# Where layer 1's second half loads its two wide tiles of x: in its tenth and thirteenth gate and up pass

## The chip, the cores and the metric

The kernel runs on one core of a Trainium2 chip. The metric is the device time of one execution in microseconds (us), of which several runs are made; their median counts. The engines are TensorE (PE), VectorE (DVE), ScalarE (ACT), GpSimd (POOL) and SyncE (SP); transfers go over 16 DMA engines, issued here mostly by SyncE ("SPq" in the profile is its queue) and by GpSimd.

## The reference

Four layers act on x, 2048 x 512 in float32, each with a norm of the rows in front and the old x added behind. Layers 0 and 2 mix by Fourier matrices, layers 1 and 3 are a gated feed-forward block with a hidden width of 1792:

```python
def _A_ref(x, dft_seq_re, dft_seq_im, dft_hid_re, dft_hid_im):
    a = jnp.einsum("bsd,ed->bse", x, dft_hid_re)
    b = jnp.einsum("bsd,ed->bse", x, dft_hid_im)
    return jnp.einsum("ts,bse->bte", dft_seq_re, a) - jnp.einsum("ts,bse->bte", dft_seq_im, b)

def _B_ref(x, w_gate, w_up, w_down):
    return (_gelu(x @ w_gate) * (x @ w_up)) @ w_down

x = x + _A_ref(_layernorm(x), ...)
x = x + _B_ref(_layernorm(x), w_gate, w_up, w_down)
x = x + _A_ref(_layernorm(x), ...)
x = x + _B_ref(_layernorm(x), w_gate, w_up, w_down)
```

## The kernel before

Every product is made of three matmuls of 128x128 by 128x512 (mm3, L213 to L215): an operand is split into a high part, which ScalarE rounds (L156), and a low part, which VectorE gets by subtraction (L158). Blocks of two by two are multiplied by Strassen's scheme (Winograd's form) with seven products instead of eight, so VectorE also adds and subtracts blocks (L189 in `minus`, L193 and L196 in `plus`), ScalarE copies finished banks of PSUM (L200 in `copied`) and writes a block into a bank as the start of a sum (L207 in `seed`). There are eight banks, p0 to p7, and 98 slots of SBUF, s0 to s97, each 128x512; both are handed out and given back as the program is written.

**Rows and layers.** x is kept in DRAM after each layer in four quarters of 512 rows: x1_2 is what layer 0 left (it is layer 1's input) of quarter 2, x2_0 what layer 1 left of quarter 0. A feed-forward layer runs in two halves (w = 0 and 1) of two quarters each. A half has 14 gate and up passes (n = 0 to 13, the function `up`), about 10 us each, in which the products of the down matrix are begun beside them (`beside`), and then the remaining down products (`down_product`, the loop over `late`). Layer 1's second half starts near 608 us, its passes end near 748, and layer 2 begins near 780. While its passes run, the norms of layer 2's rows are made ahead (`terms_ahead`): a row of x2_0 or x2_1 is loaded (L241, queue of SyncE), ScalarE sums it and its squares (L614 to L616), GpSimd takes the power (L617, L618) and ScalarE the shift (L619); later the row is loaded again and normed (L640).

**The wide tiles.** The down products come out transposed. Their result is added to x in a tile that holds a quarter of x in blocks of 32x32, turned: `xwide` for the half's first quarter (part 0, from the pool `upool`, one buffer) and `wide` for its second (part 1, from `tpool`, one buffer). `load_turned(part)` takes the tile and fills it by four loads of 256 KB on SyncE (L1508), each of 32 partitions by 16 by 128 floats, in runs of 512 bytes. `turned_into` (L801) adds a product into it on VectorE (L196), first into `xwide`, and `rows_done` writes the tile to the next layer's x.

In the program's text `load_turned(0)` is called by `beside(13)` in the last pass (k is the last pair there), and, where all seven pairs use Strassen's scheme for the down product, once more after the passes. So layer 1's halves and the first half of layer 3 load `xwide` twice with the same data: the second load waits only for the first one to land. `load_turned(1)` is called a third of the way through `late`.

**What sets the order.** The text is not the order of issue. A scheduler walks the program with its own model of time and puts an instruction on its engine's queue as soon as what it needs and the room it writes are free by that model, unless it is held by `tc.issue_after(i)`, which puts it behind the instruction i. A load needs only room, so the loads of the wide tiles go as soon as their single buffers are free, long before the place in the text. The weights are a stream of items with a look-ahead: `AHEAD` of 7 items are split ahead of use, and four more raw ones are loaded (`load_next`, L327 to L335, which notes its newest load as `stream["last"]`). On each engine, SyncE's queue among them, the instructions then run strictly in the scheduler's order. The loads of SyncE take eight completion semaphores in turn, so one is issued when the eighth before it has landed.

Of the kernel before, what the change touches and what calls it, by code (L numbers as in the profile page):

```python
# [29 lines left out]
LAG = 6  # L30
NEAR = 3, 2, 6
EARLY = 2
EARLY_FROM, EARLY_EACH = 8,2
PACE = 9
SKEW = 2, 1
# [17 lines left out]
def fnet_geglu(ctx: ExitStack, tc: tile.TileContext, x_in, ws, wh, wgu, wdn, wdc, whc, out):  # L53
# [32 lines left out]
    nc = tc.nc  # L86
# [111 lines left out]
    def copied(src):  # L198
        v = sb.get()
        bank_read["ACT"] = nc.scalar.activation(v, src, AF.Copy)  # L200
        return v
# [121 lines left out]
    stream = {"loaded": 0, "split": 0, "used": 0, "more": 0}  # L323
# [24 lines left out]
    def take():  # L348
        n = stream["used"]
        while stream["split"] < len(items):  # L350
            at = stream["split"]
            _, _, make, need = items[at]
            if too_far(at) or make is not whole and at > n + AHEAD + stream["more"]:
                break
            if make is not whole and need and need not in cs and at > n:
                break
            split_next()
        stream["used"] += 1
        return parts.pop(n)
# [126 lines left out]
    NP = NF // 2  # L486
# [308 lines left out]
    def moved(wide, outside, run):  # L795
        view = outside.rearrange("(j t) (p e) -> p t j e", t=32, e=P)
        for p in range(NT):
            v = wide[p * 32:(p + 1) * 32]
            run(v.rearrange("t (j e) -> t j e", e=P), view[p])
# [458 lines left out]
    def geglu(w, layer):  # L1258
# [12 lines left out]
        def ready(f, part):  # L1271

            t = h.get((f, part))
            if t is not None and not isinstance(t, tuple):
                h[f, part] = split_slot(t)
                sb.put(t)

        def down_steps(f, part):
# [3 lines left out]
            v = take()  # L1282
            for k in range(EARLY + 1):
                ready(f + k, part)
# [17 lines left out]
        def product(n, ps, an, bn, start, stop):  # L1302
            step()
            hi, lo = wparts[n][an]
            for c in range(2):
                cut = slice(c * P, (c + 1) * P)
                mm3(ps, (hi[:, cut], lo[:, cut]), blocks[bn, c], start and c == 0, stop and c == 1)
            if n == NF - 1:
                for c in range(2):
                    sb.put(*blocks.pop((bn, c)))  # L1310
            if an in ends:
                i = ends[an]
                sb.put(*wparts[n][i])
                if not making and n + 2 < NF:
                    piece_load(n + 2, i)
# [15 lines left out]
        def beside_mix(n):  # L1331
            run = spare.pop(0) if spare and (layer > 1 or n >= 1) else None
            if run:
                run()

        def beside_next(n, down):
            beside_mix(n)
            next(down, None)

        def up(n):  # L1340
            if n + 3 in making:
                making[n + 3][0]()
            if n + 2 in making:
                queue.extend(making[n + 2][1])
            if n > 2 or w:
                for _ in range(DOWN_RUNS[3]):
                    run = down_making.pop(0) if down_making else None
                    if run:
                        run()
            product(n, chain[n], "S2", "T2", False, True)  # L1350
            u[n] = copied(chain[n])
            down = beside(n)
            beside_next(n, down)
            side[n] = ps8.get()
            product(n, side[n], "S1", "T1", True, True)
            w4[n] = copied(side[n])
            beside_next(n, down)
            first(n + 1)
            beside_mix(n)
            product(n, chain[n], "S3", "T3", False, True)  # L1360
            v = w4.pop(n)
            plus(v, v, chain[n])
            finished(n, 1, 1, v)
            sb.put(v)
            beside_next(n, down)
            product(n, side[n], "S4", "B22", False, True)
            v = u.pop(n)
            plus(v, v, side[n])
            ps8.put(side.pop(n))
            finished(n, 0, 1, v)  # L1370
            sb.put(v)
            beside_next(n, down)
            second(n + 1)
            if pairs == NP:
                for name, k in down_order(layer, w)[1][:max(0, n - EARLY_FROM) * EARLY_EACH]:
                    if k in h4:
                        prepared(name, k)
            product(n, chain[n], "A22", "T4", False, True)
            ps = chain.pop(n)
            if n % 2 == 0:  # L1380
                v = copied(ps)
                finished(n, 1, 0, v)
                sb.put(v)
            else:
                finished(n, 1, 0, ps)
            ps8.put(ps)
            beside_next(n, down)
            for _ in down:
                pass
# [15 lines left out]
        pairs = SEVEN.get((layer, w), 0)  # L1405
# [73 lines left out]
        def beside(n):  # L1479

            if plain_down:
                return down_steps(n - LAG, 0) if n >= LAG else iter(())
            k = (n - 1) // 2
            if k >= pairs:
                return iter(())
            if n % 2:
                if k == pairs - 1:
                    load_turned(0)
                bs["A11", k] = split_slot(h[2 * k, 0])
                return down_product("A11", k)  # L1490
            if n:
                pair_combined(k)
                return down_product("A12", k)
            return iter(())

        xturned, begun = {}, {}
# [4 lines left out]
        def outside(at, part):  # L1501
            return begun[part] if at == layer + 1 and pairs < NP else xs[at, w * 2 + part]

        def load_turned(part):
            assert part or not sb.out("x")
            pool = tpool if part else upool
            xturned[part] = pool.tile([P, NT * D], F32, name="wide" if part else "xwide")
            moved(xturned[part], outside(layer, part), lambda v, rows: nc.sync.dma_start(v, rows))  # L1508

        def turned_rows(part, c, src):  # L1510
            turned_into(xturned[part], c, src)
# [15 lines left out]
        def load_rows(part):  # L1527
            xrows.extend(x_load(layer, (w * 2 + part) * NT + i) for i in range(NT))
# [72 lines left out]
                slow.pop(0)()  # L1601
        if plain_down:
            load_rows(0)
        elif pairs == NP:
            load_turned(0)
        if w == 0:
            queue.extend([None] * 9 + others[len(ahead_of_all):ND] + ([] if ahead_of_all else [None] * 4) + others[ND:])
# [3 lines left out]
        if plain_down:  # L1611
            for f in range(NF - LAG, NF):
                down(f, 0)
            add_rows(0)
            if before_mix:
                for k in range(NT):
                    queue.extend([lambda k=k: second_rows(layer + 1, k), lambda k=k: combine(k)])
                queue.extend([lambda k=k: combine_late(k) for k in range(NT)])
            else:
                queue.extend(ahead)  # L1620
            for f in range(NF):
                if f == NF - 2:
                    load_rows(1)
                down(f, 1)
                while len(queue) > 2 * (NF - 1 - f):
                    step()
            add_rows(1, before_mix)
        else:
            if pairs == NP:
                pair_combined(NP - 1)  # L1630
            late = down_order(layer, w)[1]
            for i, (name, k) in enumerate(late):
                if name == "S4" and pairs < NP:
                    break
                if pairs < NP and name == "S1" and k > 1:
                    prepared("S4", k - 2)
                for more in late[i:i + EARLY + 1]:
                    prepared(*more)
                for _ in down_product(name, k):
                    pass  # L1640
                if i == len(late) - HOLD:
                    late_end.append(newest["PE"])
                if not before_mix or i % 3 == 0:
                    step()
                if before_mix and i == len(late) // 2:
                    stream["more"] = MORE
                if i == len(late) // 3:
                    load_turned(1)
                    if w == 0:
                        queue[:2 * len(ahead)] = [run for pair in zip(ahead, queue) for run in pair] + queue[len(ahead):2 * len(ahead)]  # L1650
                while w == 0 and len(queue) > 2 * (len(late) - 1 - i):
                    step()
            if pairs < NP:
                fourth_products()
                plain_rows()
# [120 lines left out]
```

## Time and profile before

| what | us |
|---|---|
| median of three runs | 1599.49 |
| the runs | 1596.91, 1599.49, 1601.11 |
| the profiled execution's own time | 1599.44 |
| its span in the profile | 1597.5 |
| VectorE busy, share of the span | 1176.7, 74% |
| ScalarE busy, share of the span | 890.4, 56% |

One execution was recorded. A row of a timeline is one instruction, or several alike in a row: when it starts, how long it takes, its line and what it does, and in brackets how long its engine had stood idle before it and what ended that. In a group, the same figures are summed over a line. A matmul is shown as 0.39 long but the next begins 0.23 after it, since they overlap. The chain of waits goes back from the last instruction of a stretch to what released each one. The mean rate of the DMA engines over the span is 270 GB/s, and the granted clock of TensorE is at its full value throughout (all slices of the page show 9 tenths or more).

### The profile page before, as it was taken

What the parts mean: (1) busy time and instruction counts of PE and PEld (TensorE: products, weight loads), DVE (VectorE), ACT (ScalarE), POOL (GpSimd) and SP (SyncE); (2) the same over time, 40 slices, a digit from 0 to 9 for tenths busy, and PEclk for the clock granted to TensorE, in tenths of its full rate; (3) what the DMA queues carried; (4) which work ended last, traced back from release to release, by engine and by line L of the source; (5) the groups of instructions that cost most, each with busy time, mean ns of one, the idle gap of its engine ahead of it and who ended that gap; (6) DMA issues with size and microseconds to landing.
All of it is one profiled execution on the core that took longest, in us unless ns stands there. A gap on an engine that the chain in (4) does not pass through costs nothing.

```text
span 1597.5 us, 22834 instructions
## 1 busy us (share of the span) xinstructions
PE 1589.7 (100%) x6984; PEld 1310.1 (82%) x6984; DVE 1176.7 (74%) x2042; ACT 890.4 (56%) x1731; POOL 293.6 (18%) x493
## 2 busy tenths in 40 slices
PE   9999999999999999999999999999999999999999
PEld 6888888888888888788888888888888888888887
DVE  8997878888689794665879867777895557844573
ACT  8955465754767653566648545556553565333460
POOL 4112121351457101330031000001301000000000
PEclk9999999999999999999999999999999999999999
DMA  9878888996998999997895876878978968895445
GB/s 363 290 264 295 305 307 280 356 309 202 316 363 315 278 323 294 350 361 238 290 299 187 272 242 213 271 247 249 257 257 277 273 213 256 296 295 173 132 145 158
DMA packets 249433, 431.74 MB, mean 270 GB/s; under 512 B 29344, under 2 KB 74656, under 8 KB 248288
## 3 DMA queue, kind: packets, MB, share of 16 engines
q1 hardware_dynamic: 220464, 340.36, 67.3%
q0 software_dynamic: 26160, 87.84, 15.3%
q10 hardware_dynamic: 2688, 2.10, 0.5%
q8 instruction: 55, 0.90, 0.2%
q14 instruction: 66, 0.54, 0.1%
HBM read 344.46 MB, written 85.72 MB: 269 GB/s over the span
## 4 chain that ended last, share of the span: by engine, by line
PE 90%; DMA 3%; issue 3%; ACT 2%; DVE 1%; POOL 1%; SPq 0%; POOLq 0%; ACTq 0%; DVEq 0%
PE p L214 30%; PE p L213 30%; PE p L215 30%; DMA s<-t 1%; ACT s L156 1%; DVE s L158 1%; PE p L999 1%; DMA xwide<-x 1%; DMA s<-x 1%; DMA s<-ws 0%; POOL rstd L617 0%; PE p L1682 0%; ACT s L200 0%; ACT p L207 0%; DVE s L189 0%
## 5 line engine op out<-in xcount | busy, mean ns | idle before, releaser
L214 PE MATMUL p<-s,s 128*128 128x512 f32 x2312 | 897.7, 389 | 0.8 <-DVE s L158 0.8
L215 PE MATMUL p<-s,s 128*128 128x512 f32 x2312 | 892.3, 389 | 0.0
L213 PE MATMUL p<-s,s 128*128 128x512 f32 x2312 | 858.2, 389 | 1.6 <-ACT p L207 1.5
L156 ACT ACTIVATE s<-s 128x512 fp32r<-128x512 f32 (+1 forms) x859 | 483.1, 608 | 266.1 <-DVE s L189 66.9
L158 DVE TENSOR_TENSOR s<-s,s 128x512 fp32r<-128x512 f32 (+1 forms) x859 | 540.1, 663 | 111.9 <-ACT s L156 94.8
L213 PEld LDWEIGHTS p<-s,s 128*128 128x128 f32 x2312 | 433.8, 188 | 93.6 <-ACT p L207 2.6
L214 PEld LDWEIGHTS p<-s,s 128*128 128x128 f32 x2312 | 433.9, 188 | 92.1 <-DVE s L158 2.3
L215 PEld LDWEIGHTS p<-s,s 128*128 128x128 f32 x2312 | 433.9, 188 | 90.4
L193 DVE TENSOR_TENSOR s<-s,p 128x512 f32<-128x512 f32 x199 | 134.7, 683 | 163.2 <-PE p L215 136.6
L189 DVE TENSOR_TENSOR s<-s,s 128x512 f32<-128x512 f32 (+1 forms) x415 | 245.1, 612 | 4.7 <-DMA s<-ws 2.2
L200 ACT ACTIVATE s<-p 128x512 f32<-128x512 f32 x232 | 134.4, 593 | 112.6 <-PE p L215 108.5
L1253 ACT ACTIVATE s<-s 128x512 f32<-128x512 f32 x84 | 52.8, 628 | 46.4 <-DVE s L193 46.1
L617 POOL TENSOR_SCALAR rstd<-rstd 128x1 f32<-128x1 f32 x40 | 23.2, 580 | 239.3 <-ACT s L616 231.5
L1253 ACT ACTIVATE s<-p 128x512 f32<-128x512 f32 x28 | 16.7, 596 | 83.2 <-PE p L215 83.2
L319 POOL DMA_DIRECT2D wb<-s x84 | 46.2, 552 | 91.2 <-ACT s L156 68.9
L640 ACT ACTIVATE s<-s,shift,rstd 128x512 f32<-128x512 f32 x59 | 47.6, 812 | 16.9 <-DVE shift L607 9.7
L1269 DVE TENSOR_TENSOR s<-s,p 128x512 f32<-128x512 f32 x56 | 38.3, 684 | 24.7 <-PE p L215 24.7
L158 DVE TENSOR_TENSOR s<-xwide,s 128x512 fp32r<-128x512 f32 (+1 forms) x49 | 32.8, 679 | 25.2 <-ACT s L156 25.2
L196 DVE TENSOR_TENSOR s<-s,s 128x512 f32<-128x512 f32 (+1 forms) x73 | 44.2, 613 | 6.8 <-DMA s<-ws 3.8
L207 ACT ACTIVATE p<-p 128x512 f32<-128x512 f32 x56 | 32.6, 584 | 24.2 <-PE p L215 23.9
L729 DVE STREAM_TRANSPOSE wide<-s 128x512 f32<-128x512 f32 x31 | 21.9, 708 | 25.8 <-ACT s L640 21.8
L1190 POOL DMA_DIRECT2D wc<-s x42 | 30.6, 730 | 54.0 <-ACT s L156 36.3
(104 smaller groups left out, 621.8 us busy)
## 6 DMA issues: line engine op xcount, KB each, us to landing
s<-ws SPq DMA_DIRECT2D x406, 256.0 KB, 5.0
s<-wb SPq DMA_DIRECT2D x294, 256.0 KB, 5.2
s<-wc SPq DMA_DIRECT2D x182, 256.0 KB, 4.6
wb<-s POOLq DMA_DIRECT2D x98, 256.0 KB, 5.2
s<-wh SPq DMA_DIRECT2D x84, 256.0 KB, 5.3
s<-x SPq DMA_DIRECT2D x53, 256.0 KB, 5.3
wc<-s POOLq DMA_DIRECT2D x49, 256.0 KB, 5.3
xwide<-ws SPq DMA_DIRECT2D x36, 256.0 KB, 4.9
```

The source lines that it names most:

```text
L156: newest["ACT"] = nc.scalar.activation(hi, src, AF.Copy)
L158: newest["DVE"] = nc.vector.tensor_tensor(lo, src, f32(hi), op=ALU.subtract)
L189: nc.vector.tensor_tensor(out, a, b, op=ALU.subtract)
L193: bank_read["DVE"] = nc.vector.tensor_tensor(out, a, b, op=ALU.add)
L196: nc.vector.tensor_tensor(out, a, b, op=ALU.add)
L200: bank_read["ACT"] = nc.scalar.activation(v, src, AF.Copy)
L213: nc.tensor.matmul(ps, ah, bh, start=start, stop=False, skip_group_check=True)
L214: nc.tensor.matmul(ps, ah, bl, start=False, stop=False, skip_group_check=True)
L215: newest["PE"] = nc.tensor.matmul(ps, al, bh, start=False, stop=stop, skip_group_check=True)
L319: nc.gpsimd.dma_start(a, f32(t))
L640: nc.scalar.activation(z, x, AF.Identity, bias=shift, scale=rstd)
L1253: nc.scalar.activation(t, g, AF.Gelu_apprx_tanh)
```

## The change

In the second half of layer 1, `load_turned(0)` is called in the tenth pass (n = 9) and `load_turned(1)` in the thirteenth (n = 12), by a new constant `TURNED`; there the loads are held behind the stream's newest weight load by `issue_after`. `beside(13)` still loads part 0 once more. After the passes, a part that has its tile is not loaded again: that takes four loads away in the first half of layer 1 and four in that of layer 3.

```diff
+TURNED = 9, 12
@@ up(n)
             beside_next(n, down)
+            if (layer, w) == (1, 1) and n in TURNED:
+                load_turned(TURNED.index(n))
             side[n] = ps8.get()
@@ load_turned(part)
             xturned[part] = pool.tile([P, NT * D], F32, name="wide" if part else "xwide")
-            moved(xturned[part], outside(layer, part), lambda v, rows: nc.sync.dma_start(v, rows))
+            with tc.issue_after(stream["last"].ins) if (layer, w) == (1, 1) else ExitStack():
+                moved(xturned[part], outside(layer, part), lambda v, rows: nc.sync.dma_start(v, rows))
@@ after the passes
-        elif pairs == NP:
+        elif pairs == NP and not xturned:
             load_turned(0)
@@ a third into the loop over late
                 if i == len(late) // 3:
-                    load_turned(1)
+                    if 1 not in xturned:
+                        load_turned(1)
```

Lines from the second of these on stand one to five further down in the changed kernel, so L158 there is L159 and L1508 is L1512. In the rows below a name is tile_number, the number counting all tiles made; x_2_90 is x1_2, x_3_91 is x1_3, x_0_92 is x2_0 and x_1_93 is x2_1; wb and wc are weights for gate and up and for down, split already, and ws and whc matrices of layer 2.

**SyncE, first passes of layer 1's second half.** Before:

```order
L1243 DMA s_7314<-wb_146 128x512
L1508 DMA wide<-x_3_91 32x16x128 x4
L1243 DMA s_7400<-wb_146 128x512
L1243 DMA s_7399<-wb_146 128x512
L1508 DMA xwide<-x_2_90 32x16x128 x4
L333 DMA s_7356<-wc_124 128x512
L1163 DMA s_7386<-whc 128x512
...
L241 DMA s_7427<-x_0_92 128x512
L1508 DMA xwide<-x_2_90 32x16x128 x4
L241 DMA s_7430<-x_0_92 128x512
```

Between the whc load and the first row of x stand two more of whc and three of wb, left out here. In the change the twelve wide loads are gone from this place and the others keep their order.

**SyncE, tenth pass.** In the change:

```order
L334 DMA s_8068<-wc_127 128x512
L1512 DMA xwide<-x_2_90 32x16x128
L1215 DMA s_8052<-ws 128x512
L1215 DMA s_8048<-ws 128x512
L1512 DMA xwide<-x_2_90 32x16x128 x3
L1244 DMA s_8117<-wb_152 128x512
L1244 DMA s_8127<-wb_153 128x512
L1244 DMA s_8128<-wb_153 128x512
L242 DMA s_8142<-x_1_93 128x512
```

Before, the same loads stand here without the four of xwide, and the first of the three wb loads ahead of the two of ws. The loads of xwide are now ahead of the three wb loads and a row of x2_1.

**SyncE and ScalarE, last passes.** SyncE in the change:

```order
L334 DMA s_8585<-wc_127 128x512
L242 DMA s_8593<-x_0_92 128x512
L334 DMA s_8397<-wc_125 128x512
L1512 DMA wide<-x_3_91 32x16x128 x4
L1512 DMA xwide<-x_2_90 32x16x128 x4
L334 DMA s_8488<-wc_128 128x512
L334 DMA s_8550<-wc_123 128x512
L242 DMA s_8562<-x_0_92 128x512
L242 DMA s_8558<-x_0_92 128x512
L242 DMA s_8560<-x_0_92 128x512
```

All eight wide loads that the half uses or repeats stand ahead of two wc loads and three rows of x2_0. ScalarE there, before:

```order
L640 ACTIVATE s28_8564<-s19_8558,shift_7433,rstd_7432 128x512
L640 ACTIVATE s66_8595<-s69_8560,shift_7551,rstd_7550 128x512
L200 ACTIVATE s31_8462<-p5_8329 128x512
L156 ACTIVATE s71_8566<-s28_8564 128x256
L156 ACTIVATE s19_8746<-s14_7284 128x512
L640 ACTIVATE s50_8634<-s91_8562,shift_7667,rstd_7666 128x512
L156 ACTIVATE s8_8597<-s66_8595 128x256
L1253 ACTIVATE s76_8464<-s31_8462 128x512
L200 ACTIVATE s52_8495<-p7_8488 128x512
```

and in the change:

```order
L201 ACTIVATE s31_8467<-p5_8329 128x512
L641 ACTIVATE s28_8564<-s19_8558,shift_7428,rstd_7427 128x512
L641 ACTIVATE s50_8634<-s91_8562,shift_7662,rstd_7661 128x512
L1254 ACTIVATE s76_8469<-s31_8467 128x512
L641 ACTIVATE s66_8595<-s69_8560,shift_7546,rstd_7545 128x512
L201 ACTIVATE s52_8500<-p7_8493 128x512
L157 ACTIVATE s71_8566<-s28_8564 128x256
L157 ACTIVATE s19_8741<-s14_7279 128x512
```

The copies out of banks p5 and p7 stand earlier among the norms of the three rows, and the splits (L156, now L157) behind them.

**VectorE, start of layer 2.** Before, the subtraction that makes the low part in slot s46 is the last of these rows:

```order
L158 TENSOR_TENSOR s47_10101<-s5_9802,s19_10100 128x512
L158 TENSOR_TENSOR s62_10121<-s66_10052,s36_10120 128x512
L189 TENSOR_TENSOR s0_10181<-s16_10179,s0_10181 128x512
L158 TENSOR_TENSOR s83_10131<-s43_9840,s71_10130 128x512
L158 TENSOR_TENSOR s46_10138<-s49_10035,s93_10137 128x512
```

and in the change:

```order
L159 TENSOR_TENSOR s47_10096<-s5_9797,s19_10095 128x512
L159 TENSOR_TENSOR s62_10116<-s66_10047,s36_10115 128x512
L190 TENSOR_TENSOR wide_9739<-wide_9739 128x512
L159 TENSOR_TENSOR s46_10133<-s49_10030,s93_10132 128x512
L190 TENSOR_TENSOR wide_9739<-s0_10176,wide_9739 128x512
L159 TENSOR_TENSOR s79_10164<-s8_10045,s55_10163 128x512
L159 TENSOR_TENSOR s83_10126<-s43_9835,s71_10125 128x512
```

It has moved ahead of s83's, and counted from the first split of a row of `wide` (L158 with s31) it is the 26th row after instead of the 29th. Between the last passes and here 83 of VectorE's rows, 57 of TensorE's and 44 of ScalarE's have another place; outside this stretch only SyncE's queue differs, and one row of GpSimd's.

## The prediction

> **What bounds the kernel now.** I read the page's first two parts and its groups first, then the waits of TensorE, then the chain of waits, engine timelines and stretches around the three places where the change moves instructions.
>
> ```profile
> span 1597.5 us, 22834 instructions
> PE 1589.7 (100%) x6984; PEld 1310.1 (82%) x6984; DVE 1176.7 (74%) x2042; ACT 890.4 (56%) x1731; POOL 293.6 (18%) x493
> L214 PE MATMUL p<-s,s 128*128 128x512 f32 x2312 | 897.7, 389 | 0.8 <-DVE s L158 0.8
> L215 PE MATMUL p<-s,s 128*128 128x512 f32 x2312 | 892.3, 389 | 0.0
> L213 PE MATMUL p<-s,s 128*128 128x512 f32 x2312 | 858.2, 389 | 1.6 <-ACT p L207 1.5
> ```
>
> TensorE is the bound. The idle column of its three product lines adds up to 0.8 + 0.0 + 1.6 = 2.4 us in the whole span, so a change that only moves loads can win about that and no more. The change can act on TensorE only through a product that comes late. The largest wait lies in the second half of layer 1 (rows are start, duration, engine or queue, what, and in brackets the idle time before with its releaser):
>
> ```profile
> 642.95 0.39 PE L215 MATMUL p<-s,s 128*128 128x512 f32 x1
> 644.67 0.50 PE L213 MATMUL p<-s,s 128*128 128x512 f32 x1 [1.33 <-ACT p L207]
> 624.75 9.78 DMA xwide<-x
> 634.60 8.79 DMA s<-x
> 643.41 0.72 ACT s L614 x2
> 644.13 0.49 ACT p L207
> 615.99 2.78 SPq L1508 DMA_DIRECT2D wide<-x  x4
> 622.13 4.01 SPq L1508 DMA_DIRECT2D xwide<-x  x4
> 634.60 0.32 SPq L241 DMA_DIRECT2D s<-x  x1
> 635.76 3.29 SPq L1508 DMA_DIRECT2D xwide<-x  x4
> 639.36 0.42 ACT L156 ACTIVATE s<-s 128x256 fp32r<-128x256 f32 x1
> 643.41 0.63 ACT L614 ACTIVATE s<-s 128x512 f32<-128x512 f32 x1 [3.63 <-DMA s<-x]
> 621.60:634.50 12.90, 12.90 (x58) 10.68 (x58) 9.40 (x16) 4.93 (x9) 1.45 (x2) 1.00 1.15 210
> GB/s 188 192 211 208 209 192 193 202 194 181 233 298 229 163 169 195 187 195 213 216 209 197 188 208 226 182 215 304 360 384 405 397 380 392 405 427 391 372 229 156
> ```
>
> The first two rows are TensorE's: two products start 1.72 us apart, where neighbours start 0.23 apart, so 1.49 us are lost. The next four are the chain of waits: the row of x for the next norm is issued at 634.60, behind the wide loads, and takes 8.79 us to land; ScalarE, in order, stands 3.63 us for it at L614, and the seeding of a bank (L207) stands behind. The SyncE rows show what was ahead in the queue: eight wide loads, then four more. The stretch (its last number is GB/s, the one ahead of it the busy share of the DMA engines) shows 210 GB/s at a share of 1.15 while they move, against 372 in the stretch quoted below, and the slices of 621 to 640 a low of 163 among them: a wide load of 256 KB costs 256/210 = 1.25 us of transfer, a plain one 256/372 = 0.70.
>
> **Part 1: the twelve wide loads leave the first passes.** Gone from 616 to 639 are 12 issues of SyncE and 12 × 1.25 = 15 us of transfer. Nothing needs them there: the first reader is at 775.26 (below). For the row of x,
>
> ```profile
> s<-x SPq DMA_DIRECT2D x53, 256.0 KB, 5.3
> ```
>
> is the median of all such loads from issue to landing. Even issued as late as 634.60 it lands at 634.60 + 5.3 = 639.9, and ScalarE is free at 639.36 + 0.42 = 639.8. Its chain after that (0.72 + 0.49) ends at 641.2, before the 643.2 at which TensorE wants the bank. Term: −1.5 (bounds −1.5 and 0, the latter if something else is late at the same place; no other releaser stands in ScalarE's or TensorE's rows there, so I take −1.5).
>
> **Part 2: four loads of xwide in the tenth pass.** They stand behind a weight load that was issued at 699.04, interleaved with two loads of ws, and ahead of one row of x:
>
> ```profile
> 704.79 0.45 SPq L241 DMA_DIRECT2D s<-x  x1
> s<-x SPq DMA_DIRECT2D x1, 256.0 KB, 5.1
> 700.00:720.00 20.00, 20.00 (x90) 16.57 (x89) 13.46 (x22) 12.40 (x30) 7.77 (x12) 1.00 1.02 372
> 714.39 0.63 ACT L614 ACTIVATE s<-s 128x512 f32<-128x512 f32 x1 [0.76 <-PE p L215]
> 719.10 0.58 ACT L207 ACTIVATE p<-p 128x512 f32<-128x512 f32 x1
> 719.63 0.84 PE L213 MATMUL p<-s,s 128*128 128x512 f32 x3
> ```
>
> The DMA engines are full there (share 1.02), so 4 × 1.25 = 5.0 us go on top for all that is behind. The row landed at 704.79 + 5.1 = 709.9 and now lands at 714.9; ScalarE took it at 714.39, 0.5 earlier. The delay passes L614, the rest of the norm and the seeding at 719.10, which ended at 719.68; the product it feeds is the third of the TensorE row that starts at 719.63, so 719.63 + 2 × 0.23 = 720.08, 0.40 after. Late by 0.5 less 0.4: 0.1, with the unevenness of a full queue I take +0.3. Bounds: 0 (the loads slip into gaps) and +1.5 (at the 163 GB/s of that low slice a load takes 1.6 us: 6.4 in place of 5.0). The weight loads behind are, by the order, for later products than the row's, and the scheduler's look-ahead of seven items covers them.
>
> **Part 3: eight loads in the last passes.** Four of wide (the thirteenth pass) and the second four of xwide (fourteenth) stand together ahead of three rows of x for layer 1's third quarter, in a thin stretch:
>
> ```profile
> 733.00:743.00 10.00, 10.00 (x46) 8.28 (x45) 7.07 (x12) 5.05 (x9) 0.00 (x0) 1.00 0.32 82
> 733.88 0.32 SPq L241 DMA_DIRECT2D s<-x  x1
> 743.39 1.27 SPq L241 DMA_DIRECT2D s<-x  x3
> 747.26 0.82 ACT L640 ACTIVATE s<-s,shift,rstd 128x512 f32<-128x512 f32 x1 [0.99 <-DMA s<-x]
> 749.55 0.58 ACT L200 ACTIVATE s<-p 128x512 f32<-128x512 f32 x1
> 752.38 0.58 ACT L200 ACTIVATE s<-p 128x512 f32<-128x512 f32 x1
> 755.44 0.39 PE L213 MATMUL p<-s,s 128*128 128x512 f32 x1
> 775.26 0.65 DVE L196 TENSOR_TENSOR xwide<-xwide,s 128x512 f32<-128x512 f32 x1
> ```
>
> 82 GB/s of use leaves room for 2 MB in ten us: starting behind the row at 733.88, say 734.5, and with some 2 us of latency and 8 × 1.25 = 10 of transfer they land by 747 to 748.4, 27 us before VectorE first touches xwide at 775.26. The three rows queue behind their tail: I put them 3.1 to 3.7 us later, the first at about 750.7. ScalarE takes each at once (L640 at 747.26, idle 0.99 for it) and is in order, so what stands behind an L640 slips too. But its order changes: the copy out of bank p5 (before at 749.55) moves ahead of the L640s, and that of p7 (before at 752.38) ahead of four splits. Three L640 at 0.8 from 750.7, one L1253 and the p7 copy at 0.6 each end at 754.3; TensorE wants p7 again at 755.44: 1.1 to spare. The next copy, of p3, comes out 0.6 before its want. Term: 0, bounds 0 and +2 (at 1.6 us a load the eight take 2.8 us longer, less 1.1). What hides it is thus only that 1.1 and the new order.
>
> The Trainium skill says, in "DMA: Bandwidth & Descriptors", section "Rules for kernel authors", to issue a DMA early and to wait on its semaphore late; this edit does the opposite. The row at 615.99 against the use at 775.26 is that rule carried to 160 us of lead, and it is here that the early load delays another. The same page, section "Specifications", puts the least size for the full rate at 512 bytes; the wide loads are cut in such pieces and went at 210 GB/s, so the trace disagrees. By that page the eight loads would take some 5.6 us at the plain rate instead of 10, and parts 2 and 3 would cost nothing.
>
> **Part 4: the start of layer 2.** The scheduler puts VectorE's work in another order there. Before:
>
> ```profile
> 873.34 1.89 DVE L158 TENSOR_TENSOR s<-wide,s 128x512 fp32r<-128x512 f32 x3
> 890.20 1.29 DVE L158 TENSOR_TENSOR s<-s,s 128x512 fp32r<-128x512 f32 x2
> 889.64 1.07 PE L213 MATMUL p<-s,s 128*128 128x512 f32 x4
> 891.55 0.50 PE L214 MATMUL p<-s,s 128*128 128x512 f32 x1 [0.84 <-DVE s L158]
> ```
>
> TensorE runs out at 889.64 + 1.07 = 890.71 and waits for the second of the two subtractions at 890.20, which begins at 890.80. It stood 29 rows after the first row quoted, whose place is the same in the change: (890.80 − 873.34)/29 = 0.60 us a row. Now it stands 26 rows after: 873.34 + 26 × 0.60 = 888.9, done by 889.6, before 890.71. Term: −0.8. Upper bound +3: 83 rows of VectorE's order move between the last passes and here, the rows advanced push others back by about three to five places, up to 5 × 0.60 = 3.
>
> **Part 5: the second loads removed** in the first half of layer 1 and of layer 3, four each.
>
> ```profile
> 422.56 0.85 SPq L1508 DMA_DIRECT2D xwide<-x  x2
> 424.10 1.24 SPq L1508 DMA_DIRECT2D xwide<-x  x2
> ```
>
> They free 5 us of transfer where TensorE has no wait (its product lines' 2.4 us are all elsewhere or too small). Term: 0, bounds −0.2 and 0.
>
> **The sum.** −1.5 + 0.3 + 0 − 0.8 + 0 = −2.0 on the profiled execution's own 1599.44: 1597.4. The runs' median is 1599.49, the same.
>
> **Rivals.**
> 1. *The wait only moves, or layer 2's gain fails:* the 1.5 is won, but 0.8 is not and parts 2 and 3 take 1.5 together, or the stall stands again at the next row. Sum about 0: 1599.4. For it: slacks of 0.4 and 1.1 are thin. Against: both new places have a lead that was counted.
> 2. *Slower, ScalarE in the last passes:* one mechanism, the eight loads ahead of three rows that ScalarE takes in order. It decides from 10 + 1.1 = 11.1 us for the eight, 1.39 each. At 1.6 each: +1.7 there, +1.5 in the tenth pass for the same rate, −1.5: 1599.44 + 1.7 = 1601.1; with layer 2's rows late behind it another 3, 1604.1.
> 3. *Slower, layer 2's order:* VectorE is the feeder there and its 83 moved rows cost instead of win: +3 to +8 (five to thirteen rows of 0.60), less 1.2 from the first three parts, mid 1603.7. For it: TensorE already ran dry there. Against: the row it waited for moves up.
> 4. *The tiles come late for their use:* by "issue early" as the rule above has it. The last lands at 748.4 and would need to be after 775.26; each us beyond is a us, at 5 late 1602.4. 27 us speak against it.
>
> **How the numbers follow.** Forecast 0.50, rival 1 0.24, rival 2 0.13, rival 3 0.11, rival 4 0.02. A measurement of this kernel can tell about 0.3%, 4.8 us, from no change. Forecast and rival 1 lie inside; of rivals 2 to 4 about half goes past 1604.3: 0.13. Faster by 4.8 would need twice the idle time of all product rows; only the runs' own spread (1596.91 to 1601.11) gives it 0.07. Same: 0.80. Range: below, the forecast less the 2.5 by which the lowest run lies under the median, and 0.4 for the best bounds (part 2 at 0, part 5 at −0.2): 1594.5. Above, rival 3's middle: 1603.7. The forecast's own range is 1595 to 1600.
>
> **What would show it.** Right: no idle time of TensorE at L213 near 644 and ScalarE's L614 there without a long DMA wait; L214's 0.8 from L158 gone; the x row of the tenth pass landing near 715; the last wide load down by 749; the L640s of the last passes about 3 us later, with no bank wait of TensorE behind them. Wrong: a wide load longer than 1.4 us, a TensorE wait for ScalarE's L200 near 755, or a longer one for VectorE's L158 between 775 and 895.

## The result, and the profile after

| | before | the change |
|---|---|---|
| median of 13 runs each, us | 1598.42 | 1600.79 |
| lowest to highest | 1596.76 to 1601.11 | 1599.36 to 1604.16 |
| the profiled execution's own time | 1599.44 | 1599.88 |
| its span | 1597.5 | 1598.1 |

The ratio is 1.0016, with a 95% interval of 1.0009 to 1.0023: the change makes the kernel slower, by some 2.5 us. The median lies inside the whole range of the prediction (1594.5 to 1603.7) and inside its 0.3%, but above the 1595 to 1600 that it gave to its own forecast; 2.0 us of gain were forecast and the sign is the other. The profiled executions differ by 0.6 us in their spans only, so one pair of profiles does not tell the whole loss.

The page of the changed kernel, and the groups of its product lines (the columns as before; lines are one further down):

```profile
span 1598.1 us, 22799 instructions
L215 PE MATMUL p<-s,s 128*128 128x512 f32 x2312 | 896.8, 389 | 0.0
L216 PE MATMUL p<-s,s 128*128 128x512 f32 x2312 | 891.5, 389 | 0.0
L214 PE MATMUL p<-s,s 128*128 128x512 f32 x2312 | 859.5, 389 | 3.1 <-DMA s<-wb 2.0 <-ACT s L201 0.6 <-ACT s L157 0.2
```

The idle column has 3.1 us where it had 2.4. Both old releasers of size are gone: the seeding of a bank behind a row of x (1.5) and VectorE's subtraction at the start of layer 2 (0.8). Two new ones stand there. The first is a weight load. The chain of waits that leads to it, and SyncE's queue in the tenth pass:

```profile
698.13 7.72 DMA xwide<-x
705.86 7.45 DMA s<-wb
713.38 8.59 DMA s<-wb
722.01 0.50 PE p L214
```

```profile
698.13 0.90 SPq L1512 DMA_DIRECT2D xwide<-x  x1
701.92 2.56 SPq L1512 DMA_DIRECT2D xwide<-x  x3
706.35 0.37 SPq L242 DMA_DIRECT2D s<-x  x1
712.02 1.67 SPq L1244 DMA_DIRECT2D s<-wb  x3
```

```profile
722.01 0.50 PE L214 MATMUL p<-s,s 128*128 128x512 f32 x1 [1.96 <-DMA s<-wb]
```

The third of the weight loads at 712.02 is issued at 713.38 and lands at 721.97; TensorE stood from 720.05. The chain shows how it was passed on: the first wide load took 7.72 us, the loads behind wait for one of the eight completion semaphores, and each is then slow itself. ScalarE stood for the row of x that was issued at 706.35, without a wait of TensorE behind it in this execution:

```profile
714.15 0.63 ACT L615 ACTIVATE s<-s 128x512 f32<-128x512 f32 x1 [2.07 <-DMA s<-x]
```

The second new wait lies in the last passes, at ScalarE's norms of the three rows. Its timeline there, SyncE's queue, and TensorE's row:

```profile
735.44 2.01 SPq L1512 DMA_DIRECT2D wide<-x  x4
737.50 4.81 SPq L1512 DMA_DIRECT2D xwide<-x  x4
744.96 1.27 SPq L242 DMA_DIRECT2D s<-x  x3
```

```profile
753.40 1.52 ACT L641 ACTIVATE s<-s,shift,rstd 128x512 f32<-128x512 f32 x2 [5.07 <-DMA s<-x]
756.06 0.57 ACT L201 ACTIVATE s<-p 128x512 f32<-128x512 f32 x1
```

```profile
756.68 0.50 PE L214 MATMUL p<-s,s 128*128 128x512 f32 x1 [0.60 <-ACT s L201]
```

ScalarE stands 5.07 us for a row instead of 0.99, and the copy at 756.06 comes 0.6 us late. By the order of ScalarE's rows it is that of bank p7, not p3 as the first expectation below has it.

### The profile page after: what moved, and what is told of

It is laid out like the page before. It is cut to its first block, busy times and chain, and to the rows that moved or that the text cites. A ratio compares the mean times of both kernels' runs of the same rounds, so it can differ in the third digit from the quotient of the medians.

```text
span 1598.1 us, 22799 instructions
## 1 busy us (share of the span) xinstructions
PE 1589.6 (99%) x6984; PEld 1310.1 (82%) x6984; DVE 1175.4 (74%) x2042; ACT 891.4 (56%) x1731; POOL 290.0 (18%) x493
## 4 chain that ended last, share of the span: by engine, by line
PE 89%; DMA 4%; issue 4%; POOL 1%; ACT 1%; DVE 0%; SPq 0%; POOLq 0%; ACTq 0%
PE p L214 30%; PE p L216 30%; PE p L215 30%; DMA s<-wb 1%; DMA s<-t 1%; DMA s<-x 1%; DMA xwide<-x 0%; DMA s<-ws 0%; POOL rstd L618 0%; POOL wb L320 0%; ACT s L157 0%; ACT s L641 0%; POOL s L744 0%; ACT s L617 0%; POOL x L284 0%
## 5 line engine op out<-in xcount | busy, mean ns | idle before, releaser
L157 ACT ACTIVATE s<-s 128x512 fp32r<-128x512 f32 (+1 forms) x859 | 482.7, 607 | 264.4 <-DVE s L190 65.8
L159 DVE TENSOR_TENSOR s<-s,s 128x512 fp32r<-128x512 f32 (+1 forms) x859 | 539.0, 661 | 115.2 <-ACT s L157 98.5
L159 DVE TENSOR_TENSOR s<-xwide,s 128x512 fp32r<-128x512 f32 (+1 forms) x49 | 32.8, 677 | 23.6 <-ACT s L157 23.5
```

The costliest lines, as they stand in the source:

```text
L157: newest["ACT"] = nc.scalar.activation(hi, src, AF.Copy)
L159: newest["DVE"] = nc.vector.tensor_tensor(lo, src, f32(hi), op=ALU.subtract)
```

## The experiments

The theory (T): what is lost is the place of four wide loads ahead of a weight load with little lead, in a stretch where the DMA engines are full, and with it the eight wide loads of the last passes; how late each transfer lands differs from execution to execution. Every kernel was timed against the kernel before in runs on the same chip. Where a text says "order", it is that of instructions on TensorE, ScalarE and VectorE. The change, the kernel with plain loads and the one with the eleventh pass have one and the same order. The kernels without the tenth pass's loads, without the second load, and with the eleventh pass and no second load have another, common to the three; by the names and shapes in the traces it is the order of the kernel before, as is that of the kernel with the early loads once each. The kernel with late loads has a third.

| kernel | median, us | before beside it | ratio, 95% interval | span of the profile |
|---|---|---|---|---|
| the change again | 1601.66 | 1598.99 | 1.0015 (1.0006 to 1.0024) | 1600.8 |
| plain loads in the tenth pass | 1599.43 | 1598.99 | 1.0001 (0.9992 to 1.0010) | 1597.9 |
| no loads in the tenth pass | 1598.95 | 1598.99 | 0.9999 (0.9991 to 1.0008) | 1596.8 |
| no second load | 1599.27 | 1598.99 | 1.0004 (0.9995 to 1.0013) | 1598.7 |
| before again | 1598.36 | 1598.86 | 0.9998 (0.9990 to 1.0007) | 1596.0 |
| late, once each | 1601.99 | 1598.86 | 1.0017 (1.0009 to 1.0026) | 1598.0 |
| eleventh pass for the tenth | 1598.90 | 1598.86 | 1.0000 (0.9992 to 1.0009) | 1597.6 |
| early, once each | 1598.76 | 1598.86 | 1.0001 (0.9992 to 1.0010) | 1595.8 |
| eleventh pass, no second load | 1597.92 | 1598.76 | 0.9995 (0.9986 to 1.0004) | 1597.1 |
| the change a third time | 1601.37 | 1598.76 | 1.0017 (1.0008 to 1.0027) | 1597.3 |

**The change again.** No edit.

> The changed kernel once more, on another occasion. Its first profile shows two waits that the kernel before has not: 1.96 us at a product of bank p4 (722.01) for a weight load of wb that landed at 721.97, and 0.60 at 756.68 for ScalarE's copy of bank p3; the waits near 644 and 891 (1.33 and 0.84) are gone. Net of starts: +2.1 +0.8 -1.5 -1.0 = +0.4, while the runs' ratio says +2.6 us. Theory T (the wait for wb and the one in the last passes vary from execution to execution, since they hang on when transfers land): another profile shows them with another size, 1 to 5 us together, and its span follows them. Rival N (what the runs lose beyond 0.4 lies elsewhere and no profile shows it): the same 1.96 and 0.60 within 0.3, with the runs again 2 to 3 us over before.

TensorE's rows with a wait between 715 and 855, in this execution:

```profile
717.31 0.50 PE L214 MATMUL p<-s,s 128*128 128x512 f32 x1 [0.80 <-ACT s L201]
721.84 0.50 PE L214 MATMUL p<-s,s 128*128 128x512 f32 x1 [1.06 <-DMA s<-wb]
756.66 0.50 PE L214 MATMUL p<-s,s 128*128 128x512 f32 x1 [0.73 <-ACT s L201]
851.39 0.50 PE L214 MATMUL p<-s,s 128*128 128x512 f32 x1 [0.71 <-ACT s L157]
852.90 0.73 PE L216 MATMUL p<-s,s 128*128 128x512 f32 x2 [0.31 <-DVE s L159]
```

The tenth pass costs 0.80 + 1.06 = 1.86 here, split between the weight and ScalarE, which had stood for the row of x; the last passes 0.73; and the start of layer 2 now has 0.71 + 0.31 that the first profile did not have. There is also one of 0.8 for a weight load near 1374. The product lines' idle time adds up to 4.7 us against 3.1, and the span is 2.7 longer than in the first profile. The waits differ between executions, as T says.

**Plain loads in the tenth pass.** The same bytes at the same places of the queue, in runs of 2 KB:

```diff
-                load_turned(TURNED.index(n))
+                if n == TURNED[0]:
+                    dead = upool.tile([P, NT * D], F32, name="xwide")
+                    for i in range(NT):
+                        with tc.issue_after(stream["last"].ins):
+                            nc.sync.dma_start(dead[:, i * D:(i + 1) * D], xs[layer, w * 2][i * P:(i + 1) * P])
+                else:
+                    load_turned(1)
```

> The four loads of the tenth pass are made plain: 128 partitions by 512 floats, runs of 2 KB, the same bytes into the same tile at the same places of the queue; the fourteenth pass loads the tile anew, as in the change. Theory T (it is the time that the wide form takes of the DMA engines, 1.4 us a load against 0.7): the weight load lands some 2.5 us earlier, the wait for wb at 722 is gone or under 0.3, and the time falls by 2 to 3 us against the change. Rival Q (four more entries in the queue and in its eight semaphores hold what is behind, whatever their form): the wait stays at 1.5 to 2 us and the time within 1 us of the change.

The first wait of TensorE after 640 in this kernel, and the stretch of 699 to 722 in it and, below, in the change's second profile:

```profile
753.69 0.50 PE L214 MATMUL p<-s,s 128*128 128x512 f32 x1 [0.22 <-ACT s L201]
699.00:722.00 23.00, 23.00 (x103) 19.06 (x102) 17.15 (x28) 13.46 (x32) 9.16 (x13) 1.00 1.04 383
```

```profile
699.00:722.00 23.00, 21.15 (x93) 16.89 (x92) 14.78 (x24) 12.29 (x30) 6.06 (x11) 1.00 1.07 331
```

TensorE is busy 23.00 of 23 us instead of 21.15, and the DMA engines move 383 GB/s instead of 331 at the same share of time. The median is 2.2 us lower, with the same order on the engines. So it is the form of the loads that costs these 2.2 us, not four more entries in the queue: rival Q is out. The form differs in two things at once, though: runs of 512 bytes against 2 KB, and 32 partitions written by a load against 128. Which of the two it is was not tried.

**No loads in the tenth pass.**

```diff
-            if (layer, w) == (1, 1) and n in TURNED:
+            if (layer, w) == (1, 1) and n == TURNED[1]:
                 load_turned(TURNED.index(n))
```

> The change without the four loads of the tenth pass; xwide is loaded in the fourteenth pass alone, wide in the thirteenth. Theory T: no wait for wb at 722, the wait near 756 stays at 0.5 to 1.5, those of 644 and 891 stay away: 1.5 to 2.5 us faster than before. Rival L (the last passes with their eight loads cost the most, and the tenth pass little on average): 0 to 2 us slower than before, with more than 1.5 us of waits for ScalarE between 748 and 765.

The waits at 717 to 722 are gone. Two things came out otherwise than T had it. The wait near 756 is gone too, though all eight loads are still ahead of the rows:

```profile
728.88 2.02 SPq L1512 DMA_DIRECT2D wide<-x  x4
730.94 5.58 SPq L1512 DMA_DIRECT2D xwide<-x  x4
```

```profile
748.35 1.63 ACT L641 ACTIVATE s<-s,shift,rstd 128x512 f32<-128x512 f32 x2 [3.65 <-DMA s<-x]
```

They go out 6.6 us earlier than in the change (728.88 against 735.44) and the first row is there at 748.35 against 753.40. The order is that of before, so this doesn't tell the earlier place in the queue from the order. And the kernel is no faster than before: there is a wait of 0.67 for a weight load near 1168, and the one at the start of layer 2 stands again, as in the other kernels of this order:

```profile
890.17 0.50 PE L215 MATMUL p<-s,s 128*128 128x512 f32 x1 [0.87 <-DVE s L159]
```

Rival L had the time nearly right (level, where it said 0 to 2 slower), but not the waits between 748 and 765 on which it rested.

**No second load.** In `beside(13)`, `load_turned(0)` only where no tile is held yet:

```diff
-                if k == pairs - 1:
+                if k == pairs - 1 and not xturned:
                     load_turned(0)
```

> The change without the second load of xwide in the fourteenth pass: four loads in the tenth pass, four of wide in the last passes. Theory T: the wait for wb at 722 stays (2 us or more), the one near 756 goes, since the three rows of x stand behind four wide loads instead of eight and land by about 748: 0.5 to 1 us faster than the change, still 1 to 2 slower than before. Rival L: 2 us faster than the change, no slower than before.

```profile
717.32 0.50 PE L214 MATMUL p<-s,s 128*128 128x512 f32 x1 [0.39 <-ACT s L201]
721.48 0.50 PE L214 MATMUL p<-s,s 128*128 128x512 f32 x1 [0.69 <-DMA s<-wb]
```

The tenth pass's waits stay (1.08 in this execution) and none is left near 756. By the median it is 2.4 us faster than the change, more than T's 0.5 to 1 and near rival L's 2. Its order is that of before, and its interval meets that of the change, so how much the second load costs is left open. The profiled execution, at 1600.49, is 1.2 us above this kernel's median: whether its shorter ones wait in the tenth pass too was not recorded.

**Before again.** No edit.

> The kernel before, to see how far its own waits vary. Theory T: the waits near 644 (1.33) and 891 (0.84) come from the order of the queue and of VectorE and stand again within 0.5 of these sizes. Rival V: the one near 644 hangs on when a transfer lands and is mostly smaller, under 0.7, which would be why taking it away brings the runs little.

ScalarE's row for the norm, and the only wait over 0.3 of TensorE's product lines:

```profile
640.81 0.63 ACT L614 ACTIVATE s<-s 128x512 f32<-128x512 f32 x1 [0.58 <-DMA s<-x]
890.22 0.50 PE L214 MATMUL p<-s,s 128*128 128x512 f32 x1 [0.73 <-DVE s L158]
```

The row of x is there at 640.8 instead of 643.4, and TensorE doesn't wait near 644 at all: rival V, for that wait. The one near 891 stands again. So the 1.5 us that the change was to win were lost in one of the two profiled executions.

**Late, once each.** No call from `TURNED`; both tiles held behind the newest weight load, xwide in the fourteenth pass, wide a third of the way through the late products:

```diff
-            if (layer, w) == (1, 1) and n in TURNED:
-                load_turned(TURNED.index(n))
```

> No load in the tenth pass, none of the thirteenth: xwide once, in the fourteenth pass, four loads ahead of the three rows of x, and wide a third of the way through the late products, both behind the newest weight load. Theory T: no wait of TensorE between 600 and 780 above 0.3; 1 to 2.5 us faster than before. Rival O (the order that the scheduler then finds for layer 2 decides, whatever the loads do): no wait from 600 to 780, but 0.8 to 3 us of waits for VectorE's L158 or ScalarE's L156 between 840 and 900, and no faster than before.

```profile
758.86 0.42 SPq L242 DMA_DIRECT2D s<-x  x1
759.33 2.01 SPq L1510 DMA_DIRECT2D wide<-x  x4
763.71 0.43 SPq L242 DMA_DIRECT2D s<-x  x1
```

```profile
770.68 0.82 ACT L641 ACTIVATE s<-s,shift,rstd 128x512 f32<-128x512 f32 x1 [5.66 <-DMA s<-x]
774.41 0.50 PE L214 MATMUL p<-s,s 128*128 128x512 f32 x1 [1.91 <-ACT s L201]
774.20:778.60 4.40, 4.19 (x11) 3.32 (x12) 4.40 (x9) 4.40 (x10) 0.00 (x0) 0.61 1.03 366
```

Both failed: the start of layer 2 has no wait, against rival O, but a new one of 1.91 stands at 774, against T. It is T's mechanism at a place that I had not followed: four wide loads ahead of a row of x on which ScalarE stands 5.66 us, with the copy of a bank behind it. The kernel is 3.1 us slower than before.

**Eleventh pass for the tenth.**

```diff
-TURNED = 9, 12
+TURNED = 10, 12
```

> The first load of xwide is put in the eleventh pass instead of the tenth, all else as in the change: its four loads now stand behind the weight load of wb on which TensorE waited, and ahead of weights that are needed 15 us and more after they land. Theory T (it is the place of the four loads, ahead of one weight load with little lead, and not their number): the waits at 717 to 722 are gone, none takes their place before 745; about 2 us faster than the change. Rival W (the full DMA queue makes the next tight load late instead): a wait of 0.5 to 2 us for another load between 725 and 750, and within 1 us of the change.

```profile
706.97 1.65 SPq L1244 DMA_DIRECT2D s<-wb  x3
709.74 2.23 SPq L1512 DMA_DIRECT2D xwide<-x  x4
699.00:722.00 23.00, 23.00 (x103) 19.02 (x103) 16.44 (x26) 13.76 (x33) 9.31 (x14) 1.00 1.06 338
754.75 0.50 PE L214 MATMUL p<-s,s 128*128 128x512 f32 x1 [0.45 <-ACT s L201]
850.29 0.73 PE L216 MATMUL p<-s,s 128*128 128x512 f32 x2 [0.32 <-DVE s L159]
```

The loads are as many and as slow (338 GB/s), but TensorE is busy all through: the four stand behind the tight weight load, which is the third of the row at 706.97. With the same order on the engines the ratio falls from the change's 1.0015 to 1.0000, which is 2.4 us. This is the clearest evidence for the place; rival W's wait between 725 and 750 didn't come.

**Early, once each.** Before, without the load after the passes:

```diff
-        elif pairs == NP:
+        elif pairs == NP and not xturned:
             load_turned(0)
```

> The kernel before without the second load of xwide (after the passes) in layer 1 and in the first half of layer 3; the wide loads go early as before. In layer 1's second half eight wide loads still stand ahead of the row of x, the four that stood behind it are gone. Theory T: the wait near 644 stays at 1 to 1.5 and the time within 0.8 us of before. Rival D (the double loads slowed the row by sharing the DMA engines with it): the row lands 2 us or more earlier, the wait is under 0.5 and the time 1 us lower.

No wait near 644 in this execution either, as in the second profile of before; so it doesn't tell T from D. The time is that of before: the twelve loads taken out of the program as a whole bring nothing that shows.

**Eleventh pass, no second load.** The two edits together.

> The change with its first load in the eleventh pass and without the second load of xwide in the fourteenth: four wide loads behind the tight weight load, four ahead of the three rows of x. It has the same order on TensorE, ScalarE and VectorE as the kernels without the tenth pass's loads and without the second load. Theory T: no wait over 0.3 from 600 to 780; at the start of layer 2 the wait of about 1.0 for VectorE's L158 that the two others of this order show; 0 to 1 us faster than before, since the wait near 644 stood in one of two looks at before only. Rival V2 (the rest of the transfers, which differ from execution to execution, make up what is won): 0 to 1 us slower than before.

```profile
882.71 0.50 PE L215 MATMUL p<-s,s 128*128 128x512 f32 x1 [0.55 <-DVE s L159]
891.15 0.50 PE L215 MATMUL p<-s,s 128*128 128x512 f32 x1 [0.89 <-DVE s L159]
```

No wait from 600 to 780, as T has it, and 0.55 and 0.89 at the start of layer 2. It is better than the change (1.0017 on the same chip, beginning at 1.0008); against before the interval of 0.9986 to 1.0004 leaves it open whether 0.8 us are won.

**The change a third time.** No edit.

> The changed kernel a third time. Theory T: waits between 715 and 723 of 1.5 to 3 us together, near 756 of 0.5 to 0.9, and at 848 to 855 0 or 1 to 2 us; a span 1 to 5 us over the 1596.0 to 1597.5 of the two looks at before. Rival N: waits as in the first look within 0.3, the same span of 1598.

```profile
721.04 0.50 PE L214 MATMUL p<-s,s 128*128 128x512 f32 x1 [0.56 <-DMA s<-wb]
755.50 0.49 PE L214 MATMUL p<-s,s 128*128 128x512 f32 x1 [0.35 <-ACT s L201]
```

The same two places, with smaller waits than T expected; the profiled execution, at 1599.07, was the fastest of its ten. The mean span of the change's three profiles is (1598.1 + 1600.8 + 1597.3)/3 = 1598.7, that of the two of before 1596.75: 2.0 apart, where the runs say 2.4 to 2.7.

## Why the prediction was wrong

**The bound was right.** The span less the idle time of the three product lines lies between 1594.6 and 1596.2 us in all twelve profiles, while the spans themselves lie up to 5.0 apart. So the time follows the few waits of TensorE, to within 1.6 us.

**Part 1, −1.5, was mis-sized.** The mechanism was right: the row of x is issued at 625.34 in the change and ScalarE takes it at 639.77 without a wait. But the 1.49 us were those of one execution; in the second there was nothing to win. The two profiles make 0.7 on average. The step that failed is that one execution's wait was taken for the kernel's.

**Part 2, +0.3, is the step that decided.** It put the delay of all that stands behind the four loads at 5.0 us, and took the weight loads there as covered ("the scheduler's look-ahead of seven items covers them") without looking up each one's lead. The weight load on which TensorE stood is the third of this row in the kernel before:

```profile
707.92 1.68 SPq L1243 DMA_DIRECT2D s<-wb  x3
s<-wb SPq DMA_DIRECT2D x1, 256.0 KB, 5.4
```

It is issued at 709.28 and lands at 714.64, and the product that needs it starts at 721.44: a lead of 6.8 us, which a delay of 5.0 would not have used up. In the three profiles of the change the same products run 1.55, 1.91 and 1.37 us earlier here than in this one. Counted from them, the load landed 8.9, 9.1 and 7.7 us later than before, 4.4 later with plain loads and 0.1 later with the eleventh pass. So TensorE stood 1.96, 1.06 and 0.56 us for it, with ScalarE's 0.80 beside it in the second profile. By the DMA records of the trace the four wide loads take 5.4 to 5.7 us of all 16 engines there, so the 5.0 was near as transfer alone; why the delay is longer still stays open.

The row of x that I did follow was taken at 714.15, close to the 714.9 predicted, but that was luck. Part 1's gain had brought ScalarE there 1.55 us earlier, which the prediction left out: it stood 2.07 us instead of 0.76, in the second profile 3.26, where the prediction had the row 0.5 late. The plain loads and the eleventh pass, both with the change's own order, each take 2.2 to 2.4 us off the change, which is about the whole loss.

**Part 3, 0, was too low.** 0.60, 0.73 and 0.35 us in the three profiles. The mechanism was rival 2's: the rows were there at 753.4 instead of the 750.7 predicted, since the eight loads took 15.6 us from the first issue at 735.44 to the last landing at 751.02, and not the 12.5 to 13.9 of the prediction:

```profile
735.44:751.02 15.58, 15.58 (x71) 12.90 (x70) 7.69 (x12) 6.68 (x11) 0.00 (x0) 1.00 1.12 224
```

By the DMA records a wide load takes 1.6 us of all 16 engines here, a plain one 0.9; the prediction had 1.25 and 0.70, with other loads in the 210 GB/s that it divided by. 1.6 is what rival 2 put, and its 1601.1 lies near the median measured, though it put more in the last passes than is there. The order with the three L640 ahead of the copy was as predicted, and its spare 1.1 us did not suffice: in all five profiles of kernels with this order TensorE's wait is ScalarE's idle time for the row less 4.47 us (from 4.69 and 0.22 with plain loads to 5.20 and 0.73). In those two of the five that have no wide load in the tenth pass 0.22 and 0.45 are left, so the last passes lose this by themselves.

**Part 4, −0.8, was right at its place and short of the whole.** The wait near 891 is in none of the five profiles with the change's order, and stands at 0.73 to 0.89 in all six with that of before. But in the change's order 0.71 + 0.31 us stood at 851 in the second profile, 0.40 + 0.31 with plain loads and 0.32 with the eleventh pass; in the first and third nothing over 0.2 did. Rival 3 saw that VectorE's order there could give back what it wins. What decides whether this wait is there was not settled.

**Part 5, 0, held**, as far as the kernel with the early loads once each shows.

**The two rules.** The early loads cost 1.5 us in one execution of two, the late ones 1.5 in the tenth pass and 0.6 in the last passes as means of three profiles. The rule of the Trainium skill ("DMA: Bandwidth & Descriptors", section "Rules for kernel authors") to issue early and wait late would have had the sign right, but not by its reason. What came late was not the moved tiles, which were down by 751.02 and first used at 780.6, but other loads behind them; and with the loads as late as the eleventh pass the time is that of before (1.0000). Whether the 512 bytes of the same page's "Specifications" are enough for the full rate these runs do not settle: loads in such runs and plain ones differ by 2.2 us of the kernel's time in one and the same place, but also in the partitions that they write. The prediction's "the trace disagrees" holds for these loads as a whole, not for the run length alone.

**The terms as measured**, as means over the profiles: +1.5 in the tenth pass, +0.6 in the last passes, +0.3 at 851 and −0.8 at 891 in layer 2, −0.7 near 644. That makes +0.9 where the spans say +2.0 and the runs +2.5. A part of the rest stands in the granted clock, which is on record for every execution of the change: 11 of 34 have 0.999, with a median of 1602.95 us, and 23 have 1.000, with 1600.39. In the four kernels that have no wide load in the tenth pass it is 1.000 in all 44 executions. A thousandth of 1600 us is 1.6 us, about what the kernel with late loads loses in the stretch at half clock described below; 9 of its 12 executions have 0.999. But 18 of the 100 executions of the kernel before that ran beside the experiments have it too, and their median is hardly longer (1599.0 against 1598.8): the clock can also fall after the last product, as in the profile of the kernel with early loads once each (0.52 in its last 1.8 us). No profiled execution of the change has a lower clock while products run. So that its longest executions lose time to the clock after the tenth pass's wait is likely, and not shown.

## What to carry to other kernels

Where a load is put into a full queue, list every load behind it with its lead over its first use, and count the leads from where the change has moved that use; the one with the least lead decides, not the average. A wait on a transfer seen in one profile is one draw: profile twice before a gain is counted on it. When the bound engine is over 99% busy, ask first what can be made late, since nearly nothing can be won.

## What the runs showed of the hardware

Wide loads lower the rate of the DMA engines at nearly the same busy share: 331 to 338 GB/s at a share of 1.07 and 1.06 with four of them in the stretch, 383 at 1.04 with plain ones.

After the wait of 1.91 us at 774 in the kernel with late loads, products began 0.43 apart instead of 0.23 from 775.36 to 778.35, some 1.6 us lost beside the wait, and the granted clock of the stretch was 0.61. After the wait of 1.96 at 722 in the change the granted clock stayed at 1.00. The Trainium skill ("TensorE: Matmul & The Clock Gate", section "HAM oscillation — how this bites in real kernels") names idle gaps over some 3.4 us as what brings the clock down; here it fell after 1.91 and not after 1.96, so in this case the length alone does not decide.
